# A feed-forward stage in blocks of 1024 tokens: 512 columns per matmul, an output layer turned round, first-layer weights streamed

## The chip, the core and the metric

The kernel runs on one core of one Trainium2 chip. Its time is the device time of one execution in microseconds (us); the time given for a kernel is the median of its runs.

## What is computed

Three layers follow each other: a spectral layer (rfft over 3072 positions, a complex 256x256 product, a soft threshold, irfft), a top-1 mixture of eight experts, and a feed-forward layer. The change touches the third, and the loading of its weights:

```python
def _moe2_ref(x, w1, w2, w3, w_out):          # x: 24576 tokens x 256
    h = np.maximum(np.maximum(x @ w1, x @ w2), x @ w3)     # 768 features
    return (h @ w_out).astype(np.float32)                  # 256 features
```

All operands are float32.

## The kernel before

**Precision.** A float32 operand of a matmul is split in a high part (rounded to the type fp32r, by ScalarE) and a low part (the rest, by VectorE or GpSimd). A product is three matmuls into the same PSUM area: high by high, high by low, low by high.

**Stages.** `spectral` runs first. Beside its other work it decodes the feed-forward weights into `wsc`, a DRAM tensor of two parts (high, low) by 128 partitions by 9600 columns: nine units of 896 columns (seven 128x128 pieces each), then the output weights (from column `WO`). At its end `feed_weights` loads all of `wsc` into two SBUF tiles `wt`, that stay to the end. `experts` scatters its result to the DRAM tensor `xt`. `feed_forward` reads that as `xo`.

**Feed-forward.** It goes over 48 blocks of `TB` = 512 tokens, with the order of every engine's work written out by hand. A block has nine units (p, m): p is one of three groups of 256 features, m one of the three weight matrices. In a unit the 256x256 weights and the 256x512 block of tokens are each cut in 2x2 pieces, and the product is made from seven products of pieces instead of eight (the Strassen-Winograd scheme), so seven times three matmuls of 128x128 weights by 256 columns. The methods `p1`, `p52`, `p6`, `p3`, `p7`, `p4` of `Unit` are these products; L1047 issues the matmuls, into the PSUM tiles `chain` (tag pa) and `pair` (tag pb). `keep` (L1053) copies partial sums to SBUF on ScalarE, L1070 adds two of them on VectorE, L1075 one on GpSimd; `p4` takes the maximum over m (L1083, L1084 on VectorE). After m = 2, `split` makes the high part `hh` (L1092, ScalarE) and the low part `hl` (L1093, GpSimd) of the group's 1024 hidden values per partition.

The products p7 and p4 of a unit are issued within the next unit, so that the copies between them are hidden. `outputs` multiplies the hidden values of the block before by the output weights (72 matmuls of 256 columns with the hidden values as stationary operand, L1101); its matmuls are put between the products, 0, 6, 6 and then 10 in each of the nine units:

```python
done, left = last, (0, 6, 6, 10, 10, 10, 10, 10, 10)[n]
```

The result has tokens on partitions; ScalarE copies it out of PSUM (L1115) and one DMA of 512 KB a block stores it, 4 KB in a row.

`load` brings the tokens with four DMAs a block, in rows of 64 values, laid so that `prepare` needs only VectorE's 32x32 transposes (L970) to have the 256 features on partitions. `prepare` then makes the seven input combinations (L966) and their high and low parts, in steps between the units n = 2 to 6. The first block has a path of its own, `prepare_first`, with transposes on TensorE (L1010). The last block's output is `last_outputs` (L1133, L1135).

Of the kernel before, what the change touches and what calls it, by code (L numbers as in the profile page):

```python
# [113 lines left out]
def kernel(ctx: ExitStack, tc: tile.TileContext, ins, out: bass.AP):  # L114
# [24 lines left out]

    def feed_weights():  # L140
        fw = ctx.enter_context(tc.tile_pool(name="fw", bufs=1, side="right", reuse_waits="tile"))
        wt.extend(fw.tile([128, WL], F32R, name=f"fw{i}") for i in range(2))
        k = WL // 4
        for i in range(2):
            for o in range(0, WL, k):
                nc.sync.dma_start(out=wt[i][:, o:o + k].bitcast(F32), in_=wsc[i, :, o:o + k])
                yield

    wt = []
    spectral(tc, ins, rows, xt, wsc, base, small, ident, split, feed_weights(), G)  # L150
    experts(tc, ins, rows, xt, base, small, grid, ident, split, G)
    feed_forward(tc, xt, wt, ident, split, out)
# [786 lines left out]
def feed_forward(tc, xo, wt, ident, split, out):  # L939
    nc = tc.nc  # L940
    TB = 512
    NB = NT // TB
    with ExitStack() as ctx:
        st = ctx.enter_context(tc.tile_pool(name="wst", bufs=2, reuse_waits="tile"))
        ps = ctx.enter_context(tc.tile_pool(name="wps", bufs=3, space=bass.MemoryType.PSUM))
        po = ctx.enter_context(tc.tile_pool(name="wpo", bufs=2, space=bass.MemoryType.PSUM))

        xs, xts, hs, best = {}, {}, {}, {}

        def load(b):  # L950
            if b == 0:
                xs[0] = st.tile([128, 4, D], F32, tag="xs", name="xs", bufs=3)
                nc.sync.dma_start(out=xs[0], in_=xo[0:TB].rearrange("(p s) d -> p s d", s=4))
            elif b < NB:
                t = st.tile([128, 16, 64], F32, tag="xs", name="xs", bufs=3)
                v = xo[TB * b:TB * b + TB].rearrange("(s i t) (p c) -> p i t s c", i=32, t=4, p=4)
                for p in range(4):
                    nc.sync.dma_start(
                        out=t[32 * p:32 * p + 32].rearrange("i (t s) c -> i t s c", t=4), in_=v[p]
                    )  # L960
                xs[b] = t

        def prepare(b):
            if b >= NB:
                return
            sub = lambda o, i0, i1: nc.vector.tensor_tensor(out=o, in0=i0, in1=i1, op=ALU.subtract)  # L966
            x = xs.pop(b)
            xt = st.tile([128, 2, TB], F32, tag="xt", name="xt", bufs=1)
            for k in range(2):
                nc.vector.transpose(  # L970
                    out=xt[:, k].rearrange("p (s i) -> p s i", i=32), in_=x[:, :, 32 * k:32 * k + 32]
                )
                if k == 0:
                    yield
            load(b + 2)
            yield
            xh = st.tile([128, 7, 256], F32R, tag="xh", name="xh")
            xl = st.tile([128, 7, 256], F32R, tag="xl", name="xl")
            t = st.tile([128, 4, 256], F32, tag="xc", name="xc", bufs=1)
            b11, b21, b22 = xt[:, 0, 0:256], xt[:, 1, 0:256], xt[:, 1, 256:512]  # L980
            b2 = xt[:, 1].rearrange("p (a b) -> p a b", a=2)
            nc.scalar.activation(out=xh[:, 0], in_=b11, func=AF.Copy)
            sub(t[:, 1:4:2], xt[:, :, 256:512], xt[:, 0].rearrange("p (a b) -> p a b", a=2))
            nc.scalar.activation(out=xh[:, 1:3], in_=b2, func=AF.Copy)
            sub(t[:, 2], b22, t[:, 1])
            sub(t[:, 0], t[:, 2], b21)
            yield
            nc.vector.tensor_tensor(out=xl[:, 0], in0=b11, in1=xh[:, 0].bitcast(F32), op=ALU.subtract)
            nc.scalar.activation(out=xh[:, 3:7], in_=t, func=AF.Copy)
            yield  # L990
            nc.vector.tensor_tensor(out=xl[:, 1:3], in0=b2, in1=xh[:, 1:3].bitcast(F32), op=ALU.subtract)
            nc.gpsimd.tensor_tensor(out=xl[:, 3:7], in0=t, in1=xh[:, 3:7].bitcast(F32), op=ALU.subtract)
            xts[b] = xh, xl

        def prepare_first():
            sub = lambda o, i0, i1: nc.vector.tensor_tensor(out=o, in0=i0, in1=i1, op=ALU.subtract)  # L996
            def split_pool(v, h, l):
                nc.scalar.activation(out=h, in_=v, func=AF.Copy)
                nc.gpsimd.tensor_tensor(out=l, in0=v, in1=h.bitcast(F32), op=ALU.subtract)

            x = st.tile([128, 4, 2, 128], F32, tag="xs", name="xs", bufs=3)
            for j in range(4):
                (nc.vector.tensor_copy, nc.scalar.copy)[j % 2](
                    out=x[:, j].rearrange("p k (q c) -> p k q c", q=4),
                    in_=xs[0][:, j].rearrange("p (q k c) -> p k q c", q=4, k=2),
                )
            q = [po.tile([128, TB], F32, tag="t", name="t_ps") for _ in range(2)]
            for j in range(4):
                for k in range(2):
                    nc.tensor.transpose(q[k][:, 128 * j:128 * j + 128], x[:, j, k], ident)  # L1010
            load(2)
            b11, b12, b21, b22 = (a[:, o:o + 256] for a in q for o in (0, 256))
            xh = st.tile([128, 7, 256], F32R, tag="xh", name="xh")
            xl = st.tile([128, 7, 256], F32R, tag="xl", name="xl")
            t = st.tile([128, 4, 256], F32, tag="xc", name="xc", bufs=1)
            c12 = st.tile([128, 2, TB], F32, tag="xt", name="xt", bufs=1)[:, 0, 0:256]
            nc.scalar.activation(out=xh[:, 0], in_=b11, func=AF.Copy)
            nc.scalar.activation(out=c12, in_=b12, func=AF.Copy)
            sub(xl[:, 0], b11, xh[:, 0].bitcast(F32))
            sub(t[:, 1], c12, b11)  # L1020
            split(t[:, 1], xh[:, 4], xl[:, 4])
            sub(t[:, 2], b22, t[:, 1])
            split_pool(t[:, 2], xh[:, 5], xl[:, 5])
            split(b21, xh[:, 1], xl[:, 1])
            sub(t[:, 3], b22, c12)
            split_pool(t[:, 3], xh[:, 6], xl[:, 6])
            sub(t[:, 0], t[:, 2], b21)
            split_pool(t[:, 0], xh[:, 3], xl[:, 3])
            split(b22, xh[:, 2], xl[:, 2])
            xts[0] = xh, xl  # L1030

        class Unit:
            def __init__(self, b, p, m):
                self.b, self.p, self.m = b, p, m
                self.t = st.tile([128, 4, 256], F32, tag="t", name="t", bufs=4)
                self.s = st.tile([128, 4, 256], F32, tag="s", name="s", bufs=3)
                self.chain = ps.tile([128, 512], F32, tag="pa", name="pa")[:, 0:256]
                self.pair = ps.tile([128, 2, 256], F32, tag="pb", name="pb")
                if m == 0:
                    best[b, p] = self.t  # L1040

            def product(self, o, n, start, stop):
                at = 896 * (3 * self.p + self.m) + 128 * (1, 2, 6, 0, 3, 4, 5)[n - 1]
                a = [w[:, at:at + 128] for w in wt]
                v = [x[:, n - 1] for x in xts[self.b]]
                for i, (g, h) in enumerate(((0, 0), (0, 1), (1, 0))):
                    nc.tensor.matmul(  # L1047
                        o, lhsT=a[g], rhs=v[h], start=(start and i == 0), stop=(stop and i == 2),
                        skip_group_check=True,
                    )  # L1050

            def keep(self, k, o):
                nc.scalar.activation(out=self.s[:, k], in_=o, func=AF.Copy)  # L1053

            def p1(self):
                self.product(self.chain, 1, True, True)
                self.keep(0, self.chain)

            def p52(self):
                self.product(self.pair[:, 1], 5, True, True)  # L1060
                self.product(self.pair[:, 0], 2, False, True)
                self.keep(2, self.pair[:, 1])

            def p6(self):
                self.product(self.chain, 6, False, True)
                self.keep(1, self.chain)

            def p3(self):
                self.product(self.pair[:, 1], 3, False, True)
                nc.vector.tensor_tensor(out=self.t[:, 0:2], in0=self.pair, in1=self.s[:, 0:2], op=ALU.add)  # L1070

            def p7(self):
                self.product(self.chain, 7, False, True)
                self.keep(3, self.chain)
                nc.gpsimd.tensor_tensor(out=self.t[:, 2], in0=self.s[:, 2], in1=self.s[:, 3], op=ALU.add)  # L1075

            def p4(self):
                self.product(self.chain, 4, False, True)
# [141 lines left out]
```

## Time and profile before

| | |
|---|---|
| Median of 3 runs | 3067.04 us (3065.59 to 3068.78) |
| The profiled execution: its own time | 3070.35 us |
| Its span, from first to last instruction | 3068.6 us |
| TensorE matmul (PE) busy | 2919.7 us, 95% |
| TensorE weight load (PEld) busy | 2823.1 us, 92% |
| VectorE (DVE) busy | 1920.0 us, 63% |
| ScalarE (ACT) busy | 1557.4 us, 51% |
| GpSimd (POOL) busy | 1207.9 us, 39% |
| Mean granted TensorE clock | 0.978 of 2.4 GHz |

Busy time is the union of an engine's instructions; matmuls overlap in the pipeline, so that the distance of two starts tells their cost, not the length of one. Weight loads run beside matmuls. A line such as L1047 is that of the kernel before. In a wait, the name behind the arrow is what the engine waited for.

### The profile page before, as it was taken

How to read it: one execution, taken by the hardware profiler on the slowest of the kernel's cores; microseconds unless marked ns; L12 is line 12 of the kernel's file. 1: busy time of each engine (PE TensorE's matmuls, PEld its weight loads, DVE VectorE, ACT ScalarE, POOL GpSimd, SP SyncE). 2: the span in 40 equal slices, each digit the busy share in tenths (PEclk: the TensorE clock that was granted, in tenths of full speed). 3: DMA queues.
4: the chain of work that ended last, by engine and by line, in shares of the span. 5: the costliest groups of instructions: out<-in, count | busy, mean ns of one | idle time of the engine just before them, and what ended most of it. 6: DMA issues, size and time to landing. Idle time of an engine off the chain costs nothing.

```text
span 3068.6 us, 67024 instructions
## 1 busy us (share of the span) xinstructions
PE 2919.7 (95%) x23430; PEld 2823.1 (92%) x23431; DVE 1920.0 (63%) x2974; ACT 1557.4 (51%) x3530; POOL 1207.9 (39%) x1232
## 2 busy tenths in 40 slices
PE   9899989998969999999799999999999999999998
PEld 7778978977959999999799999999999999999998
DVE  6887888777744445445365666656566565666654
ACT  4444544544432333333266666666666666666664
POOL 2032223123242223222155555555555555555553
PEclk9999999999979999999899999999999999999999
DMA  5323332332343333433201111111111111111100
GB/s 149 120 70 107 107 119 63 97 114 66 118 171 91 96 100 100 126 94 96 73 22 37 35 29 42 29 43 29 29 42 29 42 29 37 34 29 42 29 29 22
DMA packets 248344, 209.77 MB, mean 68 GB/s; under 512 B 168914, under 2 KB 214566, under 8 KB 247092
## 3 DMA queue, kind: packets, MB, share of 16 engines
q1 hardware_dynamic: 233556, 179.86, 20.1%
q0 software_dynamic: 14560, 26.86, 2.4%
q8 instruction: 145, 2.38, 0.3%
q14 instruction: 83, 0.68, 0.1%
HBM read 117.77 MB, written 101.91 MB: 72 GB/s over the span
## 4 chain that ended last, share of the span: by engine, by line
PE 45%; issue 2%; DVE 2%; ACT 1%; POOL 0%; DMA 0%; POOLq 0%; SPq 0%; ACTq 0%; DVEq 0%
PE pa L1047 19%; PE pb L1047 13%; PE o_ps L1101 13%; DVE t L1084 2%; ACT s L1053 1%; PE last_ps L1101 0%; DMA xs<-xt 0%; POOLq L1216 0%; POOL hl L1093 0%; POOL t L1075 0%; ACT hh L1092 0%; PE t_ps L1010 0%; DVE t L1083 0%; ACT xh L132 0%; DVE xc L996 0%
## 5 line engine op out<-in xcount | busy, mean ns | idle before, releaser
L1047 PE MATMUL pa<-xh,fw 128*128 128x256 f32 x3456 | 763.8, 284 | 29.1 <-ACT s L1053 28.8
L1047 PEld LDWEIGHTS pa<-xh,fw 128*128 128x128 f32 x3456 | 595.0, 189 | 40.5 <-ACT s L1053 39.8
L1053 ACT ACTIVATE s<-pa 128x256 f32<-128x256 f32 x1296 | 454.7, 381 | 330.6 <-PE pa L1047 321.1
L1047 PE MATMUL pb<-xh,fw 128*128 128x256 f32 x2592 | 602.4, 281 | 0.3 <-ACT xh L132 0.3
L1093 POOL TENSOR_TENSOR hl<-t,hh 128x1024 fp32r<-128x1024 f32 x144 | 367.1, 2549 | 389.9 <-ACT hh L1092 389.9
L1047 PE MATMUL pa<-xl,fw 128*128 128x256 f32 x1728 | 485.6, 281 | 0.2 <-DVE xl L996 0.2
L1101 PE MATMUL o_ps<-fw,hh 128*128 128x256 f32 x2256 | 480.9, 281 | 0.0
L1075 POOL TENSOR_TENSOR t<-s 128x256 f32<-128x256 f32 x432 | 331.9, 775 | 338.8 <-ACT s L1053 334.0
L1070 DVE TENSOR_TENSOR t<-pb,s 128x512 f32<-128x512 f32 x432 | 293.2, 679 | 267.2 <-PE pb L1047 261.3
L1047 PEld LDWEIGHTS pb<-xh,fw 128*128 128x128 f32 x2592 | 459.1, 189 | 0.8 <-ACT xh L132 0.8
L1101 PEld LDWEIGHTS o_ps<-fw,hh 128*128 128x128 f32 x2256 | 372.8, 188 | 0.0
L1047 PE MATMUL pb<-xl,fw 128*128 128x256 f32 x1296 | 364.7, 281 | 0.0
L1047 PEld LDWEIGHTS pa<-xl,fw 128*128 128x128 f32 x1728 | 326.2, 189 | 0.4 <-DVE xl L996 0.4
L1101 PE MATMUL o_ps<-fw,hl 128*128 128x256 f32 x1128 | 317.7, 282 | 0.0
L1083 DVE TENSOR_TENSOR t<-pa,t 128x256 f32<-128x256 f32 x288 | 122.3, 425 | 286.0 <-PE pa L1047 285.9
L1084 DVE TENSOR_TENSOR t<-t 128x768 f32<-128x768 f32 x288 | 273.7, 950 | 41.4 <-POOL t L1075 41.3
L894 ACT ACTIVATE hh<-h_ps 128x512 fp32r<-128x512 f32 x208 | 120.3, 597 | 302.9 <-PE h_ps L889 288.9
L895 DVE SCALAR_TENSOR_TENSOR hl<-h_ps,hh 128x512 fp32r<-128x512 f32 x208 | 139.2, 689 | 176.7 <-ACT hh L894 156.4
L1047 PEld LDWEIGHTS pb<-xl,fw 128*128 128x128 f32 x1296 | 246.1, 190 | 0.3 <-DVE xl L135 0.3
L912 PE MATMUL y_ps<-w2l,hh 128*128 128x256 f32 x832 | 236.1, 284 | 0.9 <-POOL w2l L757 0.2
L912 PE MATMUL y_ps<-w2h,hl 128*128 128x256 f32 x832 | 235.5, 283 | 0.0
L912 PE MATMUL y_ps<-w2h,hh 128*128 128x256 f32 x832 | 235.3, 283 | 0.0
(264 smaller groups left out, 7047.2 us busy)
## 6 DMA issues: line engine op xcount, KB each, us to landing
xc<-in_x_dram SPq DMA_DIRECT2D x64, 384.0 KB
xt<-yk SPq DMA_DIRECT2D x192, 128.0 KB
xs<-xt SPq DMA_DIRECT2D x188, 128.0 KB
out_dram<-ob SPq DMA_DIRECT2D x47, 512.0 KB
xr<-rows SPq DMA_DIRECT2D x53, 264.0 KB
xs<-rows SPq DMA_DIRECT2D x208, 64.0 KB, 2.3
fw<-wsc SPq DMA_DIRECT2D x8, 1200.0 KB
w1f<-in_moe_w_dram SPq DMA_DIRECT2D x9, 1024.0 KB, 4.9
```

The costliest lines, as they stand in the source:

```text
L894: nc.scalar.activation(out=hh[:, sl], in_=p, func=AF.Relu)
L895: nc.vector.scalar_tensor_tensor(out=hl[:, sl], in0=p, scalar=0.0, in1=hh[:, sl].bitcast(F32), op0=ALU.max, op1=ALU.subtract)
L912: nc.tensor.matmul(y, lhsT=a[:, c, 128 * j:128 * j + 128], rhs=v[:, c], start=(i == 0), stop=(i == 23))
L1047: nc.tensor.matmul(o, lhsT=a[g], rhs=v[h], start=(start and i == 0), stop=(stop and i == 2), skip_group_check=True,)
L1053: nc.scalar.activation(out=self.s[:, k], in_=o, func=AF.Copy)
L1070: nc.vector.tensor_tensor(out=self.t[:, 0:2], in0=self.pair, in1=self.s[:, 0:2], op=ALU.add)
L1075: nc.gpsimd.tensor_tensor(out=self.t[:, 2], in0=self.s[:, 2], in1=self.s[:, 3], op=ALU.add)
L1083: nc.vector.tensor_tensor(out=m[:, 3], in0=self.chain, in1=m[:, 3], op=ALU.max)
L1084: nc.vector.tensor_tensor(out=m[:, 0:3], in0=m[:, 0:3], in1=self.t[:, 0:3], op=ALU.max)
L1093: nc.gpsimd.tensor_tensor(out=hl, in0=m, in1=hh.bitcast(F32), op=ALU.subtract)
L1101: nc.tensor.matmul(o, lhsT=hs[b][c // 2][g][:, (0, 3, 1, 2)[2 * (t // 2) + c % 2], 128 * (t % 2):128 * (t % 2) + 128], rhs=wo[v][:, c], st ...
```

## The change

Blocks are of 1024 tokens (`TB`), 24 of them, and each piece of tokens has 512 columns (`TH`). Every matmul of the stage has 512 columns, and there are half as many: 216 units of 21 and 24 times 72 for the output.

The output layer is turned round: the output weights are the stationary operand and the hidden values the moving one, so the result has features on partitions. It stays in four PSUM tiles (tag o) over the three groups p, is transposed by VectorE in 32x32 pieces into `ob`, and stored by eight DMAs a block, four for each half of 512 tokens, in rows of 64 values. The host permutes the columns of `w_out` to fit.

SBUF no longer holds all weights: `feed_weights` loads the output weights and the first two units; `load_unit` brings unit u + 2 into a ring of three buffers at the start of unit u. `prepare` does the same combinations on 512 columns, one piece at a time, in seven steps at n = 2 to 8; the first block uses it too, all steps at once. `split` has two parts of two pieces each, `split(0)` in the unit after the group's last and `split(1)` one unit later. The PSUM tiles pb and pc have one buffer each.

```diff
     def feed_weights():
...
+        fw["wo"] = [pool.tile([128, 6, D], F32R, name=f"wo{i}") for i in range(2)]
...
+        for u in range(2):
+            load_unit(u)
+            yield
+
+    def load_unit(u):
+        t = fw["pool"].tile([128, 2, 896], F32R, tag="wu", name="wu", bufs=3)
+        at = 896 * (u % 9)
+        nc.sync.dma_start(
+            out=t.bitcast(F32), in_=wsc[:, :, at:at + 896].rearrange("w p f -> p w f")
+        )
+        fw[u] = t
...
-    TB = 512
+    TB = 1024
+    TH = TB // 2
...
+            def high(n):
+                nc.scalar.activation(out=xh[:, n], in_=v[n], func=AF.Copy)
+
+            def low(n, e):
+                e.tensor_tensor(out=xl[:, n], in0=v[n], in1=xh[:, n].bitcast(F32), op=ALU.subtract)
+
+            sub(t[:, 1], b12, b11)
+            high(0)
             yield
+            sub(t[:, 2], b22, t[:, 1])
+            high(4)
+            low(0, nc.vector)
+            low(4, nc.gpsimd)
+            yield
             sub(t[:, 0], t[:, 2], b21)
+            high(1)
+            high(5)
+            low(1, nc.vector)
+            low(5, nc.gpsimd)
             yield
...
+            def p2(self):
+                o = ps.tile([128, TH], F32, tag="pc", name="pc")
+                self.product(o, 2, True)
+                self.add(0, o, 1)
+
+            def p5(self):
+                self.five = ps.tile([128, TH], F32, tag="pb", name="pb")
+                self.product(self.five, 5, True)
+                self.keep(5, self.five)
...
             def p3(self):
+                self.product(self.five, 3, False)
+                self.add(1, self.five, 6)
...
+                    nc.vector.tensor_tensor(out=m[:, 0:3], in0=m[:, 0:3], in1=self.t, op=ALU.max)
...
+                for i in ((0, 3), (1, 2))[part]:
+                    nc.scalar.activation(out=hh[:, i], in_=m[:, i], func=AF.Copy)
+                    nc.gpsimd.tensor_tensor(
+                        out=hl[:, i], in0=m[:, i], in1=hh[:, i].bitcast(F32), op=ALU.subtract
+                    )
...
+                        nc.tensor.matmul(
+                            o, lhsT=wo[g][:, 2 * p + c, 128 * k:128 * k + 128], rhs=h[v][:, (0, 3, 1, 2)[2 * t + c]],
+                            start=(p == 0 and i == 0), stop=(p == 2 and i == 5), skip_group_check=True,
+                        )
+                        if i == 5 and p == 2:
+                            nc.vector.transpose(
+                                out=ob[:, :, k], in_=o.rearrange("p (t i) -> p t i", i=32)
+                            )
...
+                if u + 2 < NU:
+                    load_unit(u + 2)
+                now = Unit(u)
...
+                now.p1()
+                if last:
+                    last.p7()
+                if before:
+                    before.split(1)
+                advance(it, 4)
+                now.p2()
+                now.p5()
+                if last:
+                    last.p4()
+                now.p6()
+                if last:
+                    last.split(0)
+                if n > 1:
+                    advance(pre, 1)
+                advance(it, 4)
+                now.p3()
+                before, last = last, now
```

**TensorE, one unit.** Before, in the middle of a block (pa and pb are PSUM tiles, xh and xl the parts of the tokens, fw the two weight tiles):

```order
L1047 MATMUL pb<-xh,fw_8667 128x256
L1047 MATMUL pb<-xl,fw_8667 128x256
L1047 MATMUL pb<-xh,fw_8668 128x256
L1101 MATMUL o_ps<-fw_8668,hh 128x256
L1101 MATMUL o_ps<-fw_8667,hh 128x256
L1101 MATMUL o_ps<-fw_8667,hl 128x256
L1101 MATMUL o_ps<-fw_8668,hh 128x256
L1101 MATMUL o_ps<-fw_8667,hh 128x256
L1047 MATMUL pa<-xh,fw_8667 128x256
```

In the changed kernel, from the four output matmuls behind p7 of the unit before to its p4 (wu is a unit's weights, wo the output weights):

```order
L1118 MATMUL o_ps<-hh,wo_8667 128x512
L1118 MATMUL o_ps<-hh,wo_8668 128x512
L1118 MATMUL o_ps<-hl,wo_8667 128x512 x2
L1040 MATMUL pc<-xh,wu 128x512
L1040 MATMUL pc<-xl,wu 128x512
L1040 MATMUL pc<-xh,wu 128x512
L1040 MATMUL pb<-xh,wu 128x512
L1040 MATMUL pb<-xl,wu 128x512
L1040 MATMUL pb<-xh,wu 128x512
L1040 MATMUL pa<-xh,wu 128x512
```

A unit has 29 matmuls of 512 columns now, eight of them for the output, in two lots of four.

**VectorE, the units n = 4 to 6 of a block.** Before (L1070 adds partial sums, L1083 and L1084 take maxima, L966 and L988 prepare the next block):

```order
L966 TENSOR_TENSOR xc<-xt 128x2x256
L966 TENSOR_TENSOR xc<-xt,xc 128x256
L966 TENSOR_TENSOR xc<-xc,xt 128x256
L1070 TENSOR_TENSOR t<-pb,s 128x512
L1083 TENSOR_TENSOR t<-pa,t 128x256
L1084 TENSOR_TENSOR t<-t 128x768
L988 TENSOR_TENSOR xl<-xt,xh 128x256
```

In the changed kernel (L1050 adds a partial sum, L1085 and L1086 take maxima, L978 and L999 prepare):

```order
L1050 TENSOR_TENSOR t<-pc,s_20618 128x512
L1085 TENSOR_TENSOR m<-pa,m 128x512
L1086 TENSOR_TENSOR m<-m,t 128x1536
L978 TENSOR_TENSOR xc<-xt,xc 128x512
L999 TENSOR_TENSOR xl<-xt,xh 128x512
L1050 TENSOR_TENSOR t<-pb,s_20649 128x512
L1050 TENSOR_TENSOR m<-pc,s_20670 128x512
L1085 TENSOR_TENSOR m<-pa,m 128x512
L1086 TENSOR_TENSOR m<-m,t 128x1536
L978 TENSOR_TENSOR xc<-xc,xt 128x512
L999 TENSOR_TENSOR xl<-xt,xh 128x512
L1050 TENSOR_TENSOR m<-pb,s_20701 128x512
```

The addition that frees pb (`<-pb`) stands behind the maxima and behind that unit's step of `prepare`.

**SyncE's DMA queue.** Before, a block's stores and loads:

```order
L1117 DMA out_dram<-ob 128x1024
L958 DMA xs<-xt 32x16x64 x4
```

In the changed kernel, over one block:

```order
L158 DMA wu<-wsc 128x2x896 x7
L1130 DMA out_dram<-ob 32x16x64 x4
L158 DMA wu<-wsc 128x2x896
L1130 DMA out_dram<-ob 32x16x64 x4
L158 DMA wu<-wsc 128x2x896
L972 DMA xs<-xt 32x16x64 x8
```

Nine loads of weights have joined the queue, and the stores go in rows of 64 values.

## Rows read from the trace of the kernel before

**Rows 1.** Busy time by stretch of the feed-forward stage (us; instructions; clock; DMA share; GB/s).

```profile
core 0: us, PE busy (x) PEld busy (x) DVE busy (x) ACT busy (x) POOL busy (x), PEclk, DMA share, GB/s
1522.30:1539.20 16.90, 15.60 (x90) 14.10 (x90) 8.80 (x18) 8.79 (x24) 4.33 (x6) 0.72 0.25 57
1600.00:3000.00 1400.00, 1377.82 (x11521) 1368.76 (x11521) 862.09 (x1239) 860.90 (x2074) 739.51 (x574) 1.00 0.13 34
2040.30:2062.30 22.00, 22.00 (x188) 22.00 (x187) 15.41 (x22) 13.71 (x34) 10.68 (x9) 1.00 0.00 1
```

**Rows 2.** Who waited for whom, 1600 to 3040 us, TensorE's matmuls.

```profile
PE pa L1047 <- ACT s L1053: 22.7, 45, 0.7
```

**Rows 3.** Instructions in order of time, TensorE, the head of a block (start us, us).

```profile
2037.43 0.28 PE L1101 MATMUL o_ps<-fw,hl 128*128 128x256 f32 x1
2037.55 0.28 PE L1101 MATMUL o_ps<-fw,hh 128*128 128x256 f32 x1
2038.33 0.38 PE L1047 MATMUL pa<-xh,fw 128*128 128x256 f32 x1 [0.51 <-ACT s L1053]
```

**Rows 4.** The same view in the spectral stage: four float32 matmuls of 256 columns.

```profile
83.19 1.02 PE L329 MATMUL bankD<-v,ic 128*128 128x256 f32 x4
84.05 0.59 PE L251 MATMUL bankA<-xc,f 96*128 96x512 f32 x1
```

**Rows 5.** Groups by line and shape (busy us, mean ns of one | idle before).

```profile
L1070 DVE TENSOR_TENSOR t<-pb,s 128x512 f32<-128x512 f32 x409 | 277.5, 679 | 248.3 <-PE pb L1047 247.6
L1084 DVE TENSOR_TENSOR t<-t 128x768 f32<-128x768 f32 x272 | 258.5, 950 | 38.6 <-POOL t L1075 38.5
L1083 DVE TENSOR_TENSOR t<-pa,t 128x256 f32<-128x256 f32 x272 | 115.5, 425 | 265.5 <-PE pa L1047 265.5
L970 DVE STREAM_TRANSPOSE xt<-xs 128x512 f32<-128x512 f32 x90 | 63.4, 705 | 0.0
L255 DVE STREAM_TRANSPOSE g<-bankA 128x512 f32<-128x512 f32 x46 | 45.0, 1059 | 6.3 <-PE bankA L251 5.7 <-PE bankB L251 0.6
L984 ACT ACTIVATE xh<-xt 128x512 fp32r<-128x512 f32 x45 | 28.0, 622 | 0.0
L757 POOL TENSOR_TENSOR w2l<-w2f,w2h 128x512 fp32r<-128x512 f32 x16 | 20.5, 1310 | 19.3 <-PE h_ps L889 19.1
```

**Rows 6.** In order of time, one step of the preparation: VectorE, then GpSimd.

```profile
2048.72 2.51 DVE L966 TENSOR_TENSOR xc<-xt,xc 128x256 f32<-128x256 f32 x1
...
2048.07 2.88 POOL L1093 TENSOR_TENSOR hl<-t,hh 128x1024 fp32r<-128x1024 f32 x1 [2.87 <-ACT hh L1092]
```

**Rows 7.** Transfers: weights loaded at once (by stretch), then DMA issues (KB each, us to landing).

```profile
834.00:856.00 22.00, 17.24 (x128) 16.55 (x127) 15.33 (x2) 8.39 (x11) 6.85 (x10) 0.84 1.01 420
...
w1f<-in_moe_w_dram SPq DMA_DIRECT2D x9, 1024.0 KB, 4.9
...
L958 SPq DMA_DIRECT2D xs<-xt x188: 557/636/1632, 1515.0 to 2924.7; - x188
```

**Rows 8.** In order of time, the end of the kernel.

```profile
3055.24 0.42 DVE L1083 TENSOR_TENSOR t<-pa,t 128x256 f32<-128x256 f32 x1 [5.71 <-PE pa L1047]
...
3057.68 0.58 PE L1101 MATMUL last_ps<-fw,hh 128*128 128x256 f32 x1 [2.47 <-ACT hh L1092]
...
3064.32 0.47 PE L1101 MATMUL last_ps<-fw,hh 128*128 128x256 f32 x2
...
3064.74 0.28 PE L1101 MATMUL last_ps<-fw,hh 128*128 128x256 f32 x1
3065.06 0.38 ACT L1133 ACTIVATE ob<-last_ps 128x256 f32<-128x256 f32 x1 [0.55 <-PE last_ps L1101]
```

**Rows 9.** In order of time, the start of the feed-forward stage.

```profile
1514.57 0.36 SPq L953 DMA_DIRECT2D xs<-xt  x1
...
1522.33 0.58 PE L1047 MATMUL pa<-xh,fw 128*128 128x256 f32 x1 [0.26 <-ACT xh L1017]
```

More of the change, by code (lines that the diff above doesn't have):

```diff
@@ L978, in prepare @@
[L978 to L984, printed above, removed]
+            for h in range(2):
+                x = xs.pop((b, h))
+                for k in range(2):
+                    nc.vector.transpose(
+                        out=xt[:, k, TH * h:TH * h + TH].rearrange("p (s i) -> p s i", i=32),
+                        in_=x[:, :, 32 * k:32 * k + 32],
+                    )
+                yield
@@ L989, in prepare @@
-            nc.scalar.activation(out=xh[:, 3:7], in_=t, func=AF.Copy)
+            sub(t[:, 3], b22, b12)
+            high(3)
+            high(2)
+            low(2, nc.vector)
+            low(3, nc.gpsimd)
             yield
-            nc.vector.tensor_tensor(out=xl[:, 1:3], in0=b2, in1=xh[:, 1:3].bitcast(F32), op=ALU.subtract)
-            nc.gpsimd.tensor_tensor(out=xl[:, 3:7], in0=t, in1=xh[:, 3:7].bitcast(F32), op=ALU.subtract)
+            high(6)
+            low(6, nc.gpsimd)
             xts[b] = xh, xl
[L995 to L1030, printed above, removed]
@@ L1145, in feed_forward @@
             load(0)
[L1146 to L1171 removed]
+            for _ in prepare(0):
+                pass
@@ new lines, in feed_forward @@
+            last = before = None
+            pre = it = iter(())
+            for u in range(NU):
+                b, n = divmod(u, 9)
+                if u + 2 < NU:
+                    load_unit(u + 2)
+                now = Unit(u)
+                if u >= 4 and (u - 4) % 3 == 0:
+                    it = outputs(*divmod((u - 4) // 3, 3))
+                if n == 2:
+                    pre = prepare(b + 1)
+                now.p1()
[16 more added lines that the diff above has]
+                before, last = last, now
@@ L1172, in feed_forward @@
             last.p7()
-            it = last_outputs(NB - 1)
-            next(it)
+            advance(it, 8)
             last.p4()
-            last.split()
-            next(it, None)
+            last.split(0)
+            last.split(1)
+            for i in range(2):
+                advance(it, 24)
+                if (NB - 1, 1 + i) in hs:
+                    it = outputs(NB - 1, 1 + i)
+            advance(it, 24)
 _INS = [
```

221 lines of the change are left out of this document (86 added, 135 removed).

## The prediction

> **What bounds the kernel now.** First read the busy time by stretch. Between 1600 and 3000 us TensorE starts 11521 matmuls in 1400 us, at full clock, and is busy 1377.8 us of them; no other engine is busy for more than 862 us, and the DMA engines for a share of 0.13 [rows 1]. So the stage is bound by TensorE. A block of 512 tokens has 189 matmuls for the seven products and 72 for the output, 261 in all, so it takes 1400 / 11521 x 261 = 31.72 us, and 1024 tokens take 63.43 us.
>
> Two things make up the 63.43. The first is the distance of two matmuls: between 2040.3 and 2062.3 us, a stretch without a wait, 188 matmuls stand in 22.00 us, 0.117 us each [rows 1]; the reader sees the same step from 2037.43 to 2037.55 [rows 3]. At 2.4 GHz 256 columns last 256 / 2.4 = 106.7 ns, so 10.3 ns of each are not columns. The second is a stop at the head of each block: the list of waits has 45 of them, TensorE waiting for ScalarE's copy of a partial sum [rows 2], and in order of time one shows as the step from 2037.55 to 2038.33 [rows 3]. By difference the stops cost 31.72 - 261 x 0.117 = 1.18 us a block. There, p1, p7 and the copies between them follow each other without output matmuls in between, while ScalarE waits for the maximum.
>
> **The distance of 512-column matmuls.** The trace has no fp32r matmul of 512 columns. The nearest row is a float32 matmul of 256 columns, which takes two passes of 256 with one weight load: four of them and the next matmul start at 83.19 and 84.05, so 0.215 us each, 213.3 ns of columns and 1.7 more [rows 4]. That weight load lies beside 213 ns of columns, as it will in the changed kernel, and there it costs next to nothing. I read the 10.3 ns as the price of a weight load that is hardly covered by 107 ns of columns, and take 0.2155 us for 512 columns. From below the bound is 0.2133 (columns alone); from above 0.2133 + 0.0103 = 0.2236 if those 10.3 ns belong to each matmul, and 2 x 0.117 = 0.234 if they grow with the columns.
>
> So 1024 tokens need 261 x 0.2155 = 56.25 us of matmuls against 63.43 with the stops: 7.18 us less per block of 1024, 172 us over 24, before new stops.
>
> **New stops.** A unit has 29 matmuls, 6.25 us, and its copies are twice as long as before, but the matmuls between them are too, and there are output matmuls in every unit. Count in a unit from its start: p1 ends at 0.65, p7 at 1.29, p2 at 2.80, p5 at 3.45, p4 at 4.09, p6 at 4.74, p3 at 6.25. The four copies of ScalarE at about 0.6 us (as L984) [rows 5] each have some 2 us until their reader comes. That stop goes.
>
> What is late next is VectorE, whose order is strict. Behind p4 it takes the maximum of 512 columns in PSUM, 0.68 us (as L1070), then that of 1536 columns in SBUF. L1084 and L1083 differ by 525 ns for 512 columns [rows 5], 1.03 ns a column, so 1536 take 0.95 + 768 x 1.03 ns = 1.75 us. With 0.2 us for the end of p4, VectorE is free at 6.75. Then comes that unit's step of the preparation, then the addition behind p3 (0.68 us), which frees pb, a single buffer, for p5 of the next unit, due at 6.25 + 2.80 = 9.05. A step may last 9.05 - 6.75 - 0.68 = 1.6 us.
> - n = 2: two transposes of 0.705 [rows 5] fit.
> - n = 3: two and one output transpose out of PSUM, 1.06 (as L255) [rows 5], make 2.47: 0.85 late.
> - n = 4, 7: no maximum is due in these units (m = 0), so there is room. n = 8 has nothing for VectorE.
> - n = 5: a difference and a low part, 1.36, fit if VectorE has its way.
> - n = 6: the low part needs ScalarE's high part, which queues behind two pieces of hh after 6.75: ready at 8.6, so the addition ends at 9.96: 0.9 late.
>
> That is 1.75 us a block. But a difference of two SBUF operands of 256 columns took 2.51 us where L1083 takes 0.425: it began at 2048.72, while GpSimd worked from 2048.07 to 2050.95, and ended 0.28 later [rows 6]. So it stood until GpSimd was done. In units 5 and 6 GpSimd has low parts and a sum of 512 columns, 1.31 each (as L757) [rows 5], just when VectorE has such operations. If VectorE's two in n = 5 wait for one each, the addition ends at 6.75 + 2 x 1.31 + 1.36 + 0.68 = 11.41: 2.36 late instead of 0. That gives 4.1 us a block. I take 3.0, between the two, since either engine may come first.
>
> The Trainium skill, "SBUF — State Buffer", section "Who interferes with whom", has the rule behind this row: VectorE and GpSimd share a port pair as an exclusive lock, and a VectorE operation with two SBUF inputs and a GpSimd operation block each other for a whole instruction. It speaks against this change; with it the stops would be near 4.1 us a block, without it 1.75.
>
> **Other parts.** *Weights.* A unit's 0.92 MB (128 x 2 x 896 x 4 B) joins the queue. Loading weights at once ran at 420 GB/s [rows 7], so it is 2.2 us of all DMA engines in 6.25; 1024 KB landed 4.9 us after issue [rows 7]. It may be issued once p4 of the unit before is done (4.1 us into unit u) and is needed at 12.5: it lands near 9.5. So it is hidden. Eight token loads stand between the weight loads of n = 4 and n = 5, at 0.64 us of SyncE each [rows 7], 5.1 us in all; they end before that p4 does. *Token loads and stores.* They use 0.13 x 63.43 = 8.2 us of the DMA engines per 1024 tokens now [rows 1]; if the stores in rows of 256 B double all of it, it is 16.5, and with nine units at 2.2 us 36 of 59. Hidden. *The copies of the output by ScalarE* go, VectorE's transposes come; both are off TensorE's path except as counted. *The first load of weights* shrinks from 9.8 to 3.4 MB, in a stretch where nothing waits for it: nothing.
>
> *Start.* Before, the first load went out at 1514.57 and the first product started at 1522.33 [rows 9]; by 1539.2 there were 90 matmuls in 16.9 us, 6.4 more than at 0.117 [rows 1]. Now eight loads at 0.64 go out before the last piece lands, and TensorE's transposes drop out: 1 us later, the rest alike. *End.* From the last p4 the first output matmul came after 2.44 us (3055.24 to 3057.68 [rows 8]); now 0.68 + 1.75 + 0.62 = 3.05. The clock was down until about 3064.3 [rows 8]; 24 matmuls of 512 at 0.43 and then at 0.2155 take 8.5 us instead of 7.3. Behind the last one a transpose of 1.06 and four stores issued at 0.64 replace a copy and one store: 2.9 more. 4.7 in all, of which 24 x (0.2155 - 0.117) = 2.4 are in the blocks already: about 2.
>
> **The sum.** Per 1024 tokens 63.43 - 56.25 - 3.0 = 4.18 us less, times 24 = 100.4; minus 3 at the ends = 97.4. The profiled execution took 3070.35 us in its own time (span 3068.6), so it would take 2973; it stands 3.3 above the median of the runs, 3067.04. Predicted: **2970 us**.
>
> **Rivals.**
> - *VectorE and GpSimd hardly meet:* 1.75 us of stops, 24 x 5.43 - 3 = 127 less: 2940. For it: most of GpSimd's work falls where VectorE is idle. Chance 0.20.
> - *The 10.3 ns stay with each matmul:* 0.2236, so 58.36 + 3.0 a block, 24 x 2.07 - 3 = 47 less: 3021. Rows 4 speak against it. Chance 0.10. That they grow with the columns (0.234: 61.07 + 3.0) would mean the change does not do what it says: 24 x 0.64 + 3 = 18 more, 3085. Chance 0.03.
> - *VectorE's queue becomes the bound (slower):* the place is the addition that frees pb, the price its lateness. From 7.1 us a block on the gain is gone. If in each of the seven units with a step it is late by 1.6 us, that is 11.2 a block: 24 x 4.02 + 3 = 99 more, 3167. For it: one buffer, strict order, and rows 6. Against it: units with m = 0 have 2.4 us to spare, in which it recovers. Chance 0.05.
> - *The transfers become the bound (slower):* only if the 36 us of a block become 64; at twice, 72, it is 24 x 8.6 + 3 = 209 more, 3276. Rows of 256 B are read now at little cost, but none is written in the trace. Chance 0.02. The Trainium skill, "DMA: Bandwidth & Descriptors", section "Specifications", wants 512 B and more for a transfer at line rate, with read-modify-write below; no run so far shows what a 256 B store costs.
> - *Matmuls of 512 columns come closer than their columns:* at 0.131 us each, 6264 x 0.0845 = 529 less, 2441. At 2.4 GHz 512 columns last 213 ns, and no row shows less than its columns. Chance 0.01. That figure is the sustained one of the Trainium skill, "TensorE: Matmul & The Clock Gate", section "Back-to-back issue gap"; the trace's 0.215 differs.
>
> **How the numbers follow.** My forecast has 0.57, with a range of its own from 2937 to 3000 (stops of 1.75 to 4.1 us, and a ns per matmul). The range for 8 in 10 takes in the rival below, less half of its stops and a ns a matmul (2913), and the one at 3021 with a little more stop: 2910 to 3030. It leaves out the slower cases and the tails. Within 0.2%, 6 us, a measurement of this kernel can't tell a change from none. Faster: 0.57 + 0.20 + 0.10 + 0.01 = 0.88. Slower: 0.03 + 0.05 + 0.02 = 0.10. The 0.02 left lie between, the same.
>
> **What would show it.** Right: four-in-a-row matmuls of the stage 0.2155 us apart; the stops at the block's head gone, and instead TensorE waiting for VectorE before matmuls into pb, after n = 3, 5 and 6, some 3 us a block; a DMA share near 0.6; no wait for wu. Wrong: a step of 0.224 or more; TensorE waiting for wu's landing; waits before pb in every unit; or VectorE's differences at their plain 0.7 us and no waits at all.

## The result and the profile after

The changed kernel took **3028.23 us** (median of 4 runs, 3026.91 to 3034.47) against 3066.32 us for the kernel before on the same chip: a ratio of 0.988, 95% interval 0.986 to 0.990. That is 38 us less, where 97 were predicted. The profiled execution took 3028.35 us in its own time, with a span of 3026.6.

First the stage as a whole. The view by stretch of the changed kernel, 1600 to 3000 us (busy time and number of instructions of each engine, granted clock, DMA share):

```profile
1600.00:3000.00 1400.00, 1393.59 (x5903) 1107.95 (x5903) 873.10 (x1011) 741.61 (x1308) 769.22 (x563) 1.00 0.60 167
```

1400 / 5903 = 0.2372 us for a matmul of 512 columns with all stops in it, 61.9 us for the 261 of a block of 1024 tokens. Before, 1400 / 11521 x 522 = 63.4 [rows 1]. So a block gained 1.53 us, not 4.18; 24 of them are 37 of the 38. By the starts of the matmuls, stops between them were 0.83 us in a block of 512 before and are 0.78 us in a block of 1024 now, which is 0.9 of the 1.53; the other 0.65 is the step, 0.2343 against twice 0.1184 us. TensorE is busy for all but 6.4 of the 1400 us at full clock, so what is left is not idle time. The DMA share is 0.60, as foreseen.

Then the step, in order of time, TensorE, in a stretch without a wait:

```profile
2012.72 0.39 PE L1040 MATMUL pb<-xh,wu 128*128 128x512 f32 x1
2012.95 0.39 PE L1040 MATMUL pb<-xl,wu 128*128 128x512 f32 x1
2013.18 0.40 PE L1040 MATMUL pb<-xh,wu 128*128 128x512 f32 x1
2013.42 0.40 PE L1040 MATMUL pa<-xh,wu 128*128 128x512 f32 x1
2013.66 0.39 PE L1040 MATMUL pa<-xl,wu 128*128 128x512 f32 x1
2013.89 0.63 PE L1040 MATMUL pa<-xh,wu 128*128 128x512 f32 x2
2014.36 0.39 PE L1040 MATMUL pa<-xl,wu 128*128 128x512 f32 x1
2014.59 0.39 PE L1040 MATMUL pa<-xh,wu 128*128 128x512 f32 x1
2014.82 1.10 PE L1118 MATMUL o_ps<-hh,wo 128*128 128x512 f32 x4
2015.76 0.40 PE L1040 MATMUL pb<-xh,wu 128*128 128x512 f32 x1
```

From 2012.72 to 2015.76 there are 13 steps of **0.234 us**, products and outputs alike. The prediction had 0.2155; 0.234 is twice the 0.117 read before [rows 1, 3]. By the trace's starts the ordinary step is 0.2343 in every part of the stage.

Last the waits of TensorE (matmuls and weight loads) from 1600 to 3000 us:

```profile
PE pb L1040 <- DVE m L1050: 5.6, 22, 0.3
PE pb L1040 <- DVE t L1050: 0.8, 1, 0.8
PEld pb L1040 <- DVE m L1050: 15.2, 22, 0.7
PEld pb L1040 <- DVE t L1050: 10.0, 23, 1.2
```

The stop at the block's head [rows 2] is gone. A new one stands where it was expected, before matmuls into pb, waiting for VectorE's addition; it comes in two units of a block (p5 of n = 7 and of n = 6; the shorter one shows in the weight loads alone). The distance from the matmul ahead is then 0.65 and 0.36 us instead of 0.234, and 0.1 us more behind each: about 0.76 us a block, not 3.0. No row waits for wu.

### The profile page after: what moved, and what is told of

Same layout as the page of the kernel before. It is cut to its first block, busy times and chain, and to the rows that moved or that the text cites. A ratio compares the mean times of both kernels' runs of the same rounds, so it can differ in the third digit from the quotient of the medians.

```text
span 3026.6 us, 53435 instructions
## 1 busy us (share of the span) xinstructions
PE 2891.4 (96%) x17158; PEld 2502.2 (83%) x17159; DVE 1919.2 (63%) x2707; ACT 1407.6 (47%) x2657; POOL 1222.3 (40%) x1206
## 4 chain that ended last, share of the span: by engine, by line
PE 45%; DVE 3%; ACT 1%; issue 1%; DMA 0%; SPq 0%; POOL 0%; DVEq 0%
PE pa L1040 18%; PE o_ps L1118 12%; PE pb L1040 10%; PE pc L1040 4%; DVE m L1086 1%; ACT hh L1097 1%; DVE xl L999 1%; DVE m L1050 0%; ACT xh L996 0%; DVE xc L978 0%; DMA xs<-xt 0%; SPq L972 0%; POOL hl L1098 0%; DVE xt L983 0%; DVE t L1050 0%
## 5 line engine op out<-in xcount | busy, mean ns | idle before, releaser
L1040 PE MATMUL pa<-xh,wu 128*128 128x512 f32 x1728 | 616.8, 397 | 19.5 <-ACT xh L996 19.2
L1047 ACT ACTIVATE s<-pa 128x512 f32<-128x512 f32 x648 | 378.6, 595 | 339.4 <-PE pa L1040 216.4
L1098 POOL TENSOR_TENSOR hl<-m,hh 128x512 fp32r<-128x512 f32 x288 | 398.0, 1403 | 301.4 <-ACT hh L1097 301.4
L1040 PEld LDWEIGHTS pa<-xh,wu 128*128 128x128 f32 x1728 | 326.1, 189 | 99.7 <-ACT xh L996 19.4
L1040 PE MATMUL pb<-xh,wu 128*128 128x512 f32 x864 | 348.3, 403 | 7.4 <-DVE m L1050 5.9
L1040 PE MATMUL pa<-xl,wu 128*128 128x512 f32 x864 | 343.2, 397 | 3.7 <-DVE xl L999 3.7
L1118 PE MATMUL o_ps<-hh,wo 128*128 128x512 f32 x1152 | 340.7, 398 | 3.4 <-ACT hh L1097 3.4
L1086 DVE TENSOR_TENSOR m<-m,t 128x1536 f32<-128x1536 f32 x144 | 251.7, 1748 | 0.0
L902 PE MATMUL h_ps<-xh,w1h 128*128 128x256 f32 x832 | 230.1, 277 | 1.6 <-DVEq L884 1.6
L902 PE MATMUL h_ps<-xl,w1h 128*128 128x256 f32 x832 | 230.1, 277 | 0.0
L1050 DVE TENSOR_TENSOR t<-pc,s 128x512 f32<-128x512 f32 x144 | 99.3, 689 | 167.3 <-PE pc L1040 137.1
```

The source lines that it names most:

```text
L902: nc.tensor.matmul(p[:, j], lhsT=a[:, k, f0:f0 + 128], rhs=v[:, k], start=(i == 0), stop=(i == 5))
L1040: nc.tensor.matmul(o, lhsT=self.w[:, g, at:at + 128], rhs=v[h], start=(start and i == 0), stop=(i == 2), skip_group_check=True,)
L1047: nc.scalar.activation(out=self.s[k], in_=o, func=AF.Copy)
L1050: nc.vector.tensor_tensor(out=self.t[:, i], in0=o, in1=self.s[k], op=ALU.add)
L1086: nc.vector.tensor_tensor(out=m[:, 0:3], in0=m[:, 0:3], in1=self.t, op=ALU.max)
L1098: nc.gpsimd.tensor_tensor(out=hl[:, i], in0=m[:, i], in1=hh[:, i].bitcast(F32), op=ALU.subtract)
```

## The experiments

The open question was why 512 fp32r columns take 0.234 us.

### Matmuls alone: what sets the step

The edit is a new program: one matmul shape behind the other, each block of 84 or more with one thing changed.

```
for i in range(N):
    nc.tensor.matmul(o(i), lhsT=zr[:, 0:128], rhs=zr, **s(i))    # L194
for i in range(N):
    nc.tensor.matmul(o(i), lhsT=w(i, wb), rhs=xb, **s(i))        # L208
```

> A program of matmuls alone (the model's result is not computed; the output is filled with zeros). Blocks of 84 or more fp32r matmuls stand one behind the other without waits, each block with one thing changed: 512, 496, 384, 256 and 128 columns; no sums in PSUM; one weight; one moving operand; one PSUM bank; zeros as operands; bf16; float32 of 256 columns; and 512 columns beside work of ScalarE, VectorE, GpSimd, or transfers into and out of SBUF. Theory A (fp32r columns are slower in themselves, about 1.1 cycles each): 512 columns take 0.234 us in every block, 256 take 0.117, 384 take 0.176, and bf16 takes 0.215. Theory B (the weight load takes SBUF reads from the moving operand, or every matmul has a fixed price): the price for a column falls from 256 to 512 columns, and the block with one weight is no different from a new weight each time. Theory C (neighbours): 512 columns take 0.2155 us when the other engines rest, and 0.234 or more only beside ScalarE, VectorE, GpSimd or transfers. Theory D (the data): with zeros 512 columns take 0.2155 us, with numbers 0.234. Theory E (PSUM): one bank, or no sums, changes the step.

Groups by line (busy time, mean ns of one), and then one stretch, the block of 512 fp32r columns with numbers:

```profile
L194 PE MATMUL p<-zr 128*128 128x512 f32 x84 | 19.2, 389 | 0.0
L208 PE MATMUL p<-xb,wb 128*128 128x512 bf16 x84 | 18.3, 379 | 0.0
L210 PE MATMUL p<-v 128*128 128x256 f32 x168 | 36.4, 379 | 0.0
```

```profile
52.80:71.70 18.90, 18.90 (x85) 15.63 (x85) 0.00 (x0) 0.00 (x0) 0.00 (x0) 1.00 0.00 1
```

The busy time is that of 83 steps and one whole matmul. So fp32r with zeros has a step of (19.2 - 0.389) / 83 = 0.2266 us, and bf16 (18.3 - 0.379) / 83 = 0.2159. With numbers, the 84 starts of the block give 0.2267; the stretch shows x85 because it counts a matmul that reaches over its edge too. (The 0.117 read from a short stretch of before [rows 1] has this error, about 1%; its step is 0.1184 over products and outputs, and the stops of before were 0.83 us a block, not the 1.18 that the prediction took by difference.) The last line is the 84 float32 matmuls of 256 columns: 168 records, 0.216 us apart.

No sums, one weight, one moving operand, one bank, zeros: 0.2267 each. Beside ScalarE, VectorE, GpSimd and transfers the median stays 0.227. So C, D and E fall. 256 columns take 0.120 us, 384 take 0.173: with 512 all three are 13.3 ns above their columns at 2.4 GHz (106.7, 160 and 213.3), as B has it, and against A. But a fixed 13 ns can't be what the kernels have: 256 columns take 0.117 to 0.118 there, less than here, and 512 take 0.234, more than here. One block gave a hint: 496 columns that began 64 bytes further on took 0.2273, 20.6 ns above their columns.

### 512 columns, or only the blocks and the order

```
-    nc.tensor.matmul(o, lhsT=self.w[:, g, at:at + 128], rhs=v[h], ...)
+    for c in (slice(0, 256), slice(256, 512)):
+        nc.tensor.matmul(o[:, c], lhsT=self.w[:, g, at:at + 128], rhs=v[h][:, c], ...)
```

The output's matmuls are cut alike. The start flag stands on both halves of a bank, and there the sum of the first half loses its first product; number and kind of the instructions are the same.

> After, with each matmul of 512 columns issued as two of 256 on the same weights, loaded for each: the blocks of 1024 tokens, the order of the work and the streamed weights stay, the 512 columns per weight load go. If the price grows with the columns (step 0.117 to 0.118 us for 256), 6264 x (2 x 0.1184 - 0.2343) = 16 us more: 3044. If a fixed price of 10 ns stood in each matmul, 6264 x 0.0103 = 65 more: 3093. If the gain of the change came all from the 512 columns, 3066 as before.

3037.43 us, ratio 0.993 (0.991 to 0.995) to before. Of the change's 1.2%, the blocks, the order and the streamed weights alone bring 0.7%; the 512 columns bring the other half per cent, some 16 us (12 by the length of the stage in the two traces). The plain step of the halves is 0.1177 us, twice that 1.1 ns more than 0.2343. So the first of the three cases came, and at this place no fixed 10 ns stands in each matmul.

### Twice the transfers

```
-    nc.sync.dma_start(out=t.bitcast(F32), in_=wsc[...])
+    for _ in range(2):
+        nc.sync.dma_start(out=t.bitcast(F32), in_=wsc[...])
```

> After, with each unit's weights transferred twice into the same buffer: 216 more transfers of 896 KB, 2.2 us of all DMA engines each. If the transfers are hidden and do not slow TensorE's columns: 3028, within 6 us, the step of 512 columns stays 0.234. If transfers into SBUF are what makes the columns slow, the step grows by as much again as they made it, up to 0.25: 3028 + 6264 x 0.02 = 3150. If the weights land late, TensorE waits for wu.

3423.75 us, ratio 1.119 (1.117 to 1.122): the third case, and far more than expected. The list of waits and the view by stretch:

```profile
PE pa L1041 <- DMA wu<-wsc: 254.9, 145, 6.7
PEld pa L1041 <- issue: 225.2, 92, 7.1
```

```profile
1700.00:3300.00 1600.00, 1343.53 (x5297) 1033.50 (x5295) 787.86 (x914) 680.09 (x1177) 680.01 (x508) 0.95 0.77 237
```

TensorE now waits for wu. Between the waits, where the clock is full (0.95 of it on average), its ordinary step is still 0.234, at a DMA share of 0.77, so transfers don't make the columns slow. In the changed kernel one load takes 3.1 to 3.9 us from its first packet to its last and lands 4 to 5 us after its issue, of 6.8 us in a unit; the prediction had 2.2 us of transfer. Doubled into the same buffer, the second waits for the first to land, and the two need about 8 us. So the weights are hidden, with less room than the prediction's sum says.

### The place of the operands in SBUF

In this program 512 columns differ only in how many bytes the weights and the moving operand lie past one address.

```
for m in mm(512, 0, 0):        # L146: weights + 0, moving + 0
    nc.tensor.matmul(**put(m))
...
for m in mm(512, 352, 256):    # L186: as in the changed kernel
    nc.tensor.matmul(**put(m))
```

> A program of matmuls alone again (the model's result is not computed; the output is mostly zeros). In the run before, 512 fp32r columns took 226.7 ns with all operands at multiples of 64 bytes, while the kernel's step is 234.3; its streamed weights and output weights lie at 32 bytes past a multiple of 64, its tokens at a multiple. Here 36 blocks of 101 matmuls differ only in how many bytes the weights and the moving operand lie past a fixed address (0 to 384). Theory F (the place of the weights): with weights 352 bytes on and the moving operand 256 on, as in the kernel, the step is 234 ns; with both at multiples of 64 it is 227 or less; for 256 columns 117 to 118 against 113 or 120. Rival G (something else of the kernel, its waits, engines or the number of its instructions): every block with 512 columns takes 226.7 ns, whatever the address. Rival H: only the moving operand's place counts, the weights' does not.

Groups by line (the step is busy time less the mean of one, over 100):

```profile
L186 PE MATMUL p<-x,w 128*128 128x512 f32 x101 | 23.8, 396 | 0.0
...
L188 PE MATMUL p<-x,w 128*128 128x512 f32 x101 | 23.7, 396 | 0.0
...
L182 PE MATMUL p<-x,w 128*128 128x512 f32 x101 | 23.1, 389 | 0.0
...
L146 PE MATMUL p<-x,w 128*128 128x512 f32 x101 | 23.1, 389 | 0.0
...
L190 PE MATMUL p<-x,w 128*128 128x256 f32 x101 | 12.3, 283 | 0.0
...
L212 PE MATMUL p<-x,w 128*128 128x256 f32 x101 | 12.0, 280 | 0.0
L210 PE MATMUL p<-x,w 128*128 128x256 f32 x101 | 11.6, 276 | 0.0
```

| line | columns | weights, moving (bytes on) | distance modulo 256 | step, us |
|---|---|---|---|---|
| L186 | 512 | 352, 256 (the changed kernel) | 96 | 0.234 |
| L188 | 512 | 320, 256 | 64 | 0.233 |
| L182 | 512 | 256, 256 | 0 | 0.227 |
| L146 | 512 | 0, 0 | 0 | 0.227 |
| L190 | 256 | 0, 0 | 0 | 0.120 |
| L212 | 256 | 352, 256 (the products of before) | 96 | 0.117 |
| L210 | 256 | 384, 320 | 64 | 0.113 |

Theory F holds, G and H fall: neither address alone decides, but the distance of the two. Moved together by 32, 64 or 256 bytes, 512 columns stay at 0.227; moved apart by 32 to 224 bytes they take 0.229 to 0.234. At the kernel's distance the successive steps repeat the kernel's own: 231, 234, 235, 233, 232, 237, 238 ns, and again. The places that are good for 256 columns are others: distance 0 is the worst there. That the reads of the next matmul's weights and of this one's columns from SBUF get in each other's way would fit, but the runs show only the dependence. The Trainium skill, "TensorE: Matmul & The Clock Gate", section "Step-by-step: what each phase is for", says that loading the next weights takes no read bandwidth from the running matmul; here the place of the weights alone moves the step from 0.227 to 0.234, which that sentence does not let one expect; which read is slowed, no run shows.

### The same in the kernels

One unused tile behind the weights' pool moves all weights down. In the changed kernel 96 bytes bring distance 0; in the two others 32 bytes bring 64.

```
         for u in range(2):
             load_unit(u)
             yield
+        pool.tile([128, 24], F32, name="pad")
```

> After, with one unused tile of 96 bytes a partition behind the weights, so that the streamed and the output weights lie 96 bytes lower, at the same place modulo 256 as the tokens and the hidden layer. Theory F (the step depends on where the weights lie against the moving operand): the step falls from 234.3 to 226.7 ns, 6264 x 7.6 ns = 47.6 us less, 3028 - 48 = 2980; the waits for VectorE may give back some us, since each unit is 0.22 us shorter. Rival G: the step stays at 234.3, 3028.

2987.21 us, ratio 0.977 (0.975 to 0.978). By stretch, and the waits from 1600 to 2800 us:

```profile
1600.00:2800.00 1200.00, 1188.87 (x5189) 970.71 (x5188) 778.89 (x893) 654.51 (x1156) 685.92 (x499) 1.00 0.61 172
```

```profile
PE pb L1041 <- DVE m L1051: 8.3, 20, 0.4
```

1200 / 5189 = 0.2313 us with stops instead of 0.2372. The step fell from 0.2343 to 0.2271, and the waits before pb grew, as each unit is 0.2 us shorter. The stage, from the first product to the last output matmul, went from 1502.5 to 1466.8 us: of 48 us foreseen, 36 came. (The medians differ by 41, but the kernel before was 6 us faster on this chip.) This shows in the kernel itself that the place costs 7.2 ns a matmul, since the instructions and their order are the same and only the weights lie 96 bytes lower. Some 13 ns above the columns are left, as in the program of matmuls alone at its best places; no run takes them away.

The 256 columns in the new order, with `[128, 8]` for the tile (and one start flag for a bank):

> After, with each matmul of 512 columns issued as two of 256 on the same weights, loaded for each, and an unused tile of 32 bytes behind the weights, so that these stand 64 bytes from the moving operands modulo 256. Theory F: a step of 113.4 ns for 256 columns, as cheap per column as 512 at their best place (226.7): 3028 - 6264 x (234.3 - 226.8) = 2981, the same as with 512 columns well placed: the 512 columns per weight load bring nothing of their own. Rival (a price for each matmul is left that 512 columns halve): at least 10 ns for each of 6264 more matmuls, 63 us, 3044 or more.

3001.78 us, ratio 0.982 (0.980 to 0.984), and a step of 0.1137. Two of them are 0.2274, as against 0.2271 for 512 columns well placed. So 512 columns per weight load save next to nothing in the step, once each has its best place: 2 us over all matmuls. The medians differ by 15 us, 3001.78 against 2987.21; the spans of the two profiled executions, 2995.1 and 2984.1, differ by 5 us ahead of the stage and by 6 in it, 2 of them in the step and the rest in stops. The rival's 63 us are not there.

And the kernel before, with the same small tile behind its `fw`:

> Before, with one unused tile of 32 bytes a partition behind its weights, so that they lie 32 bytes lower and the products' weights stand 64 bytes from the tokens modulo 256. Theory F: the products' step falls from 118.4 to 113.4 ns, 9072 x 5.0 = 45 us less, the output's from 119.4 to 117.8, 3456 x 1.6 = 6 less: 3067 - 51 = 3016, so all of the change's gain without its 512 columns. If the stops at the block's head grow by what the matmuls save, less of it is left. Rival G: 3067.

3047.12 us, ratio 0.996 (0.994 to 0.997): 13 us, not 51; the stage is 16 us shorter in the trace. The products' step fell from 0.1181 to 0.1169 us on average, not to 0.1134. In order of time it has two levels at the same places, 0.114 and 0.118:

```profile
2004.91 0.28 PE L1048 MATMUL pa<-xh,fw 128*128 128x256 f32 x1
...
2005.60 0.28 PE L1102 MATMUL o_ps<-fw,hh 128*128 128x256 f32 x1
...
2005.94 0.28 PE L1048 MATMUL pb<-xh,fw 128*128 128x256 f32 x1
...
2007.71 0.28 PE L1102 MATMUL o_ps<-fw,hh 128*128 128x256 f32 x1
```

Six products take 0.69 us here, and the fifteen behind the next output matmuls 1.77. The output's matmuls have the hidden layer as weights and `wo` as the moving operand, so they are at a distance of 192, for which the program above gave 0.118 (256 columns, 0 and 64). Here they keep the level of the products ahead of them, 0.113 or 0.118, about half of them each; where products follow again, the level changes in nine cases of ten. So the table of the program does not carry over to matmuls whose distance alternates, and what sets the level stays open. This shift does not give before all that the change gives; other shifts, or a shift of the hidden layer by itself, were not tried.

### The stop before pb

```
             high(5)
-            low(1, nc.vector)
             low(5, nc.gpsimd)
 ...
             low(6, nc.gpsimd)
+            low(1, nc.vector)
```

> After, with VectorE's low part of one operand taken from the preparation step of unit n = 6 to that of n = 8. If the stop before pb comes from that low part, which waits for ScalarE's high part behind two pieces of the hidden layer: 23 stops of 0.7 to 0.75 us go, 16 to 17 us less, 3011. If VectorE is late for its maximum and difference alone, half of it stays: 3020. If what is moved makes the next block's first unit late, a new stop stands there: 3028 or more.

3015.94 us, ratio 0.985 (0.984 to 0.987). From the first product to the last output matmul it is 1495.7 us against 1502.5. By the trace's starts the stop at n = 7 went, 0.5 us in each of 23 blocks; that at n = 6 stayed, since its low part was not moved; and the first block, which has no unit to hide in, waited 3 us longer for the low part that now comes last. So between the first and the second case: the low part of n = 6 was most of the stops, not all.

Both together, with the low part of n = 5 moved to n = 7 as well:

> After, with both: the unused tile of 96 bytes behind the weights, and VectorE's two low parts taken one unit later (n = 5 to n = 7) and two units later (n = 6 to n = 8). In the run with the tile alone the stops before pb grew to 0.58 and 0.30 us a block (n = 7 and n = 6), with 0.1 us behind each: 23 x 1.08 = 25 us that should go, so 2987 - 25 = 2962. If VectorE's queue is late in these units for another reason, 2987 stays; if the low parts make the next block's first units late, more than 2987.

2982.11 us, ratio 0.974 (0.972 to 0.975). The stops before pb went, but the last case came beside the first: TensorE stopped before the next block's second product for the late low part, 10 us in all, and the first block was late by 5 at its start. The wait from 1600 to 2800 us:

```profile
PEld pc L1041 <- DVE xl L1000: 10.8, 20, 0.6
```

> After, with the unused tile of 96 bytes behind the weights, and VectorE's low parts moved only for blocks behind the first: those of n = 5 and n = 6 to n = 7, where no maximum is due, and that of n = 7 to n = 8, which the next block needs last. In the run before, the low part in n = 8 was late for the next block's second product (10 us of stops over the blocks) and the first block started 5 us later. If these were the moves' own price, the stops before pb and before pc are gone: 2982 - 10 - 5 = 2967. If three low parts in n = 7 are late for its addition, a stop before pb at n = 8 takes their place: 2980.

2963.95 us, before 3049.09 on that chip: ratio **0.972** (0.971 to 0.974), ahead of the changed kernel (0.988) and of the tile alone (0.977).

```profile
1600.00:2800.00 1200.00, 1194.88 (x5237) 978.79 (x5236) 830.10 (x902) 652.57 (x1163) 704.33 (x501) 1.00 0.62 174
```

```profile
PE pb L1049 <- DVE t L1059: 5.1, 20, 0.3
```

1200 / 5237 = 0.2291 us, 2 ns above the plain step. Some of the second case came too: a wait before pb once a block, at the next unit (n = 0) behind the low part of n = 8. From the first product to the last output matmul the stage takes 1453.3 us, against 1459.0 in the run before and 1466.8 with the tile alone. But 3.4 of these last 5.7 us are the first block's start, and from 1600 to 2800 us the stops add up to 10.6 us against 12.7. So the stops have moved for the most part, and few are gone. The median agrees with the 2967 expected, but the kernel before was 16 us faster on this chip as well; by the ratios, 0.972 and 0.974, the gain on the run before is 0.1%, which their intervals do not tell from none.

## Why the prediction was wrong

- **What bounds the kernel** was right: TensorE, before and after.
- **The distance of 512-column matmuls is the step that failed.** It read the 10.3 ns beyond the columns as a weight load that is hardly covered and took 0.2155 us from a float32 row [rows 4]. Measured: 0.2343, the upper bound it had kept with a chance of 0.03. 6264 x 18.8 ns = 118 us. The float32 row was the nearest by shape, but in the program of matmuls alone 84 float32 matmuls of 256 columns stand as 168 records of 0.216 us. So the four records of [rows 4], there called four matmuls, are two, and a record takes 518 cycles of 2.4 GHz for 256 columns, about two each; the trace can't tell slow columns from two passes. Either way the row did not tell what 512 fp32r columns cost. Nor do the runs bear out the other half of the step, the 10.3 ns as a weight load without cover (11.7 ns, with the step at 0.1184): at the kernel's place they became 20.9 ns with 512 columns, and two loads with 256 columns cost no more than one with 512 once each is well placed. Of the 18.8 ns that the sum lacked, 7.2 hang on where the weights lie; the cause of the other 11.6 stays open: in the program of matmuls alone bf16 keeps 2.6 ns above its columns, fp32r with 512 columns never less than 13.3.
- **New stops** were over-sized: 3.0 us a block against 0.76, below the lower bound of 1.75, which gives 54 us back. The order of VectorE shows why.

```profile
1807.56 0.69 DVE L1085 TENSOR_TENSOR m<-pa,m 128x512 f32<-128x512 f32 x1 [0.65 <-PE pa L1040]
1808.17 1.75 DVE L1086 TENSOR_TENSOR m<-m,t 128x1536 f32<-128x1536 f32 x1
1809.83 1.78 DVE L978 TENSOR_TENSOR xc<-xt,xc 128x512 f32<-128x512 f32 x1
1811.54 0.68 DVE L999 TENSOR_TENSOR xl<-xt,xh 128x512 fp32r<-128x512 f32 x1
1812.14 0.68 DVE L1050 TENSOR_TENSOR t<-pb,s 128x512 f32<-128x512 f32 x1
...
1816.86 0.68 DVE L978 TENSOR_TENSOR xc<-xc,xt 128x512 f32<-128x512 f32 x1
1818.68 0.85 DVE L999 TENSOR_TENSOR xl<-xt,xh 128x512 fp32r<-128x512 f32 x1 [1.14 <-ACT xh L996]
1819.45 0.68 DVE L1050 TENSOR_TENSOR m<-pb,s 128x512 f32<-128x512 f32 x1
```

```profile
1809.45 1.61 POOL L999 TENSOR_TENSOR xl<-xc,xh 128x512 fp32r<-128x512 f32 x1 [2.92 <-ACT xh L996]
```

  The maximum of 1536 columns takes 1.75 us, as worked out. In n = 5 the difference takes 1.78 us beside GpSimd and 0.68 alone: the wait for GpSimd of [rows 6] is there. The Trainium skill, "SBUF — State Buffer", section "Who interferes with whom", calls the port pair that the two share an exclusive lock, and these rows agree. But only one of two operations meets it, and the addition ends at 1812.82: of the 2.36 us of lateness about 0.1 is left. In n = 6 the low part does wait for ScalarE's high part (1.14 us); it is 0.4 late instead of 0.9. In n = 3 nothing is late: the output transpose out of PSUM took 0.705 us, not the 1.06 of another shape [rows 5]. And each unit lasts 29 x 18.8 ns = 0.55 us longer than in the sum, which is room for VectorE; with the step at 0.227 the stops grew by half.
- **Weights, token loads, stores:** hidden, as said, with a share of 0.60. One load takes 3.1 to 3.9 us of the queue instead of 2.2, and no wait for the 256 B stores shows.
- **The ends.** The first product started 4.9 us earlier (1517.47 against 1522.33 [rows 9]), not 1 later: the experts' last matmul started 2.8 earlier, and from there it was 19.5 us instead of 21.6. The 2.8 are not the stage's doing: in later runs with the same experts that matmul starts between 1482 and 1501 us. Behind the last matmul there are 6.6 us instead of 3.8, close to the 2.9 more that were worked out.
- **The sum with what was measured:** 97 - 118 + 54 + 6 for the start = 39. The profiled executions differ by 42, the medians by 38. That the kernel still became faster, and lies 2 us inside the range, is luck: the step alone, with the stops as forecast, is the rival of 3085, and the over-sized stops gave back nearly half of what the step took.

## What to carry to other kernels

When a matmul's step is longer than its columns, find out what the rest depends on before scaling it to a longer matmul: a price per matmul halves, a price per column doubles, and a row of another type cannot tell them apart. With fp32r operands, look where the stationary and the moving operand lie against each other in SBUF, modulo 256 bytes; an unused tile of 96 bytes was worth about as much here (ratio 0.988 to 0.977) as the rewrite (1 to 0.988). And a lateness that was summed from durations on one engine needs the other engine's longer unit in the same sum.

## What had not been expected of the hardware

- 512 fp32r columns take 0.227 to 0.234 us, 256 take 0.113 to 0.120, by the distance of weights and moving operand modulo 256 bytes; bf16 takes 0.216 for 512 at the places tried.
- With 256 columns the same placement can run at 0.113 or at 0.118 us. In the kernel before with the small tile the level changes where products follow the output's matmuls.
- 128 fp32r columns take 0.111 us, hardly less than 256 at their best.
